# Moving three load slots 224 bytes up in each partition of a decode kernel

## The chip, the core and the metric

The kernel runs on one core of a Trainium2 chip. The metric is the device time of one execution in microseconds (us). Before the change the median of three executions is 1370.03 us, from 1369.99 to 1370.04 us.

## What is computed

One token passes through a parallel block of a transformer: layer norm, then attention over a long cache beside a gated feed-forward, and both are added to the input. Everything is fp32.

```python
xn   = layernorm(x)                                # x: [1, 1, 576]
q    = (xn @ wq).reshape(1, 1, 32, 128)            # 32 heads of 128
s    = einsum("bhqd,bhkd->bhqk", q, k_cache) * 128 ** -0.5   # k_cache: [1, 32, 16384, 128]
p    = softmax(s)
o    = einsum("bhqk,bhkd->bhqd", p, v_cache)       # v_cache: [1, 32, 16384, 128]
attn = o.reshape(1, 1, 4096) @ wo                  # wo: [4096, 576]
ffn  = (gelu(xn @ w_gate) * (xn @ w_up)) @ w_down  # 576 -> 4608 -> 576
out  = x + attn + ffn
```

There is one query, so every element of the caches is used once. K and V are 8.39 MB each for a head, 537 MB for the 32 heads; with the weights the core reads 587.6 MB from device memory.

## The kernel before

**The slots.** Nearly all that is loaded goes to three buffers of 65,536 bytes in each of the 128 partitions: two K slots (`kpool`, names `kslot`) and one V slot (`vpool`, name `vslot`). One slot holds the K or the V of one head: 128 positions of 128 floats in a partition. The slots lie one behind another. The lowest begins at byte 27,680 of the partition, the next two at 93,216 and 158,752. Below them lies the pool `cpool` with the small tiles that live for the whole program, above them `spool` with the small tiles of a head. All pools are laid out in the order in which the program opens them, each tile at the next multiple of 32 bytes.

**The loads.** Every load of a cache or a weight is issued by `load()` (L69) on SyncE's DMA queue. A transfer of a head's K or V is 128 rows, one for each partition, of 65,536 contiguous bytes each; the destination begins where the slot begins. The first head's K comes in two halves. The weights share the slots: `wq` and the feed-forward's `w_gate` and `w_up` come first (parts of `w_gate` and `w_up` in the V slot, name `mix`), `w_down` and `wo` come last. Their parts begin at places within a slot that are multiples of 256 bytes.

**The head loop** (from L249 on). For head h it issues the load of K of head h, then the load of V of head h-1, and then:

- `qk` (L215, L216): VectorE multiplies K in place by the query, which lies in all partitions in the tile `qs`, and sums over the 128 elements of each position into the scores `s`.
- `pv` of the head before (L236): 64 matmuls on TensorE with the weights of the softmax in the tile `pe` and V as the moving operand, summed in PSUM.
- `softmax` (L220 to L229): the maximum over partitions by way of TensorE, then one exponential on ScalarE, which writes `pe` and, through `accum_out`, the row sum into column h of the tile `lsum`.

A load waits on SyncE's queue until its slot is free. The V slot is free when `pv` is done. A K slot is free when `qk` of two heads earlier is done; by the order of issue that load also follows the load of V before it. The DMA queue itself works through what has been issued in order, so a load that is issued while another is still moving starts when that one is through.

**The end.** `w_down` and `wo` are loaded in pieces that get smaller, the last ones 2,304 bytes in a partition. TensorE multiplies each piece as it lands (L281), `lsum` is summed over partitions at L300, and 576 floats are written out.

**Where the small tiles lie.** `lsum` is the second last tile of `cpool` ahead of the head loop: behind it follow `oall`, three small tiles of the feed-forward's activation and three of the end (`rl`, `on`, `oT`), and behind those the slots.

```python
lsum = cpool.tile([P, H], F32, name="lsum")
oall = cpool.tile([P, H], F32, name="oall")
```

Of the kernel before, what the change touches and what calls it, by code (L numbers as in the profile page):

```python
# [8 lines left out]
F32 = mybir.dt.float32  # L9
# [4 lines left out]
P = 128  # L14
H, SK, DH = 32, 16384, 128
# [19 lines left out]
QUART = D // 4  # L35
HG = 4
PW = 4 * HG
QH = 4


@with_exitstack
def kernel(ctx: ExitStack, tc: tile.TileContext, x, k_cache, v_cache, wq, wo, wg, wu, wd, out):
    nc = tc.nc
    cpool = ctx.enter_context(tc.tile_pool(name="cpool", bufs=1))
# [17 lines left out]
    def kslot():  # L62
        return kpool.tile([P, R * DH], F32, tag="k", name="kslot")

    def vslot():
        return vpool.tile([P, R * DH], F32, tag="v", name="vslot")

    def load(dst, src):
        nc.sync.dma_start(dst, src)  # L69
        return dst  # L70
# [79 lines left out]
    def q_spread(h):  # L150
        r = 32 * (h // (H // 4))
        lo = h % (H // 4) * DH
        pq = ps_s.tile([P, 512], F32, tag="sm", name="pq")
        nc.tensor.matmul(pq, ones[r : r + 1, :], qrow[r : r + 1, lo : lo + QH * DH], start=True, stop=True)  # L154
        return pq

    def q_take(h, pq):
        qs = spool.tile([P, QH, DH], F32, name="qs", bufs=1)
        nc.scalar.activation(qs.rearrange("p h d -> p (h d)"), pq, AF.Copy)
        for i in range(QH):  # L160
            Q[h + i] = qs[:, i : i + 1, :]
# [41 lines left out]
    S, KT, VT = {}, {}, {}  # L203
    pe = cpool.tile([P, PW - 4 + 32 * PW], F32, name="pe")
    nc.vector.memset(pe, 0.0)
    pe4 = pe[:, PW - 4 :].rearrange("p (k s) -> p k s", s=PW)[:, :, :4]
    lsum = cpool.tile([P, H], F32, name="lsum")
    oall = cpool.tile([P, H], F32, name="oall")

    def qk(h, i, n):  # L210
# [21 lines left out]
    def pv(h):  # L232
        vt, i = VT.pop(h), h % HG
        for k in range(32):
            q, lo = 32 * (k % 4), k * PW + PW - 4 - 4 * i
            nc.tensor.matmul(PO[h // HG % 2][q : q + PW, :], pe[:, lo : lo + PW], vt[:, k * 512 : (k + 1) * 512],  # L236
                             start=i == 0 and k < 4, stop=i == HG - 1 and k >= 28)

    def out_heads(h):
        o4 = spool.tile([P, 512], F32, name="o4", bufs=1)  # L240
        nc.scalar.activation(o4, PO[h // HG % 2], AF.Copy)  # L241
        pc = ps_s.tile([P, 512], F32, tag="sm", name="pc")
        pick = same[:, :PW].rearrange("p (i j) -> p j i", j=4)
        for j in range(4):
# [4 lines left out]
    for h in range(H + 1):  # L249
# [4 lines left out]
        if h > 0:  # L254
            VT[h - 1] = load(vslot() if h < H else kslot(), vv[h - 1])
        more = (h + 1) % QH == 0 and h + 1 < H
        pq = q_spread(h + 1) if more else None
# [100 lines left out]
```

## Time and profile before

| what | value |
|---|---|
| median of 3 executions | 1370.03 us |
| the profiled execution's own time | 1370.16 us |
| its span, first to last instruction | 1368.3 us |
| VectorE busy | 1135.8 us (83%) |
| TensorE matmuls busy | 406.0 us (30%) |
| mean busy share of the 16 DMA engines | 9 tenths or more in 39 of 40 slices |
| bytes moved by DMA, mean rate | 588.00 MB, 430 GB/s |
| packets on the loads' queue | 11,664 |

The span leaves 1.86 us of the profiled execution outside it. An engine is busy while one of its instructions runs; idle time of an engine that is not the bottleneck costs nothing. A packet of the DMA queue is one contiguous row of a transfer, or a four-byte one that tells a semaphore that an engine's part is done. A rate taken over a short stretch is rough, since a packet's bytes are put down to its own time.

### The profile page before, as it was taken

To read this page: it belongs to the slowest core of one execution; us is meant where nothing else is said; L and a number is where in the kernel's file an instruction comes from. 1 tells how busy PE (TensorE), PEld (TensorE's weight loads), DVE (VectorE), ACT (ScalarE), POOL (GpSimd) and SP (SyncE) were. 2 spreads that over 40 slices of the span, in tenths; PEclk is the share of its full clock that TensorE was granted. 3 is DMA by queue.
4 is the path that set the end of the run, shared out by engine and by line. 5 is a ranking of instruction groups with operands and counts; after the bars stand their busy time and mean duration, and the time that the engine had idled before them with its cause. 6 is when DMAs were issued, how large, how long until landed. Compare 5 with 4: busy or idle time off the path is not lost.

```text
span 1368.3 us, 6377 instructions
## 1 busy us (share of the span) xinstructions
PE 406.0 (30%) x2870; PEld 118.1 (9%) x2870; DVE 1135.8 (83%) x169; ACT 36.5 (3%) x126; POOL 1.0 (0%) x7
## 2 busy tenths in 40 slices
PE   4321233322311232323212332322213333221156
PEld 1110000100000000100000000100001000000012
DVE  1069999899888888898888888998888888988840
ACT  0000000000000000000000000000000000000000
POOL 0000000000000000000000000000000000000000
PEclk8775565565556556565566566565556555665577
DMA  9999999999999999999999999999999999999997
GB/s 404 440 425 450 430 429 430 430 435 432 437 435 429 431 430 439 432 432 435 431 436 433 433 431 430 435 432 439 435 430 430 431 432 437 438 435 428 429 428 336
DMA packets 11704, 588.00 MB, mean 430 GB/s; under 512 B 1303, under 2 KB 1309, under 8 KB 1694
## 3 DMA queue, kind: packets, MB, share of 16 engines
q1 hardware_dynamic: 11664, 587.60, 99.4%
q8 instruction: 22, 0.36, 0.1%
q14 instruction: 4, 0.03, 0.0%
q10 hardware_dynamic: 14, 0.01, 0.0%
HBM read 587.60 MB, written 0.00 MB: 429 GB/s over the span
## 4 chain that ended last, share of the span: by engine, by line
DMA 51%; DVE 46%; PE 2%; issue 0%; SPq 0%; ACT 0%; DVEq 0%
DMA kslot<-in_A_k_cache_dram 41%; DVE s L216 23%; DVE kslot L215 23%; DMA kslot<-in_A_v_cache_dram 3%; DMA kslot<-in_B_w_up_dram 3%; DMA kslot<-in_A_wo_dram 3%; DMA kslot<-in_A_wq_dram 2%; PE pg L139 1%; PE po L236 1%; DVE gu L179 0%; SPq L69 0%; PE pt L222 0%; DVE vslot L176 0%; DVE pm L220 0%; DVE nm L224 0%
## 5 line engine op out<-in xcount | busy, mean ns | idle before, releaser
L215 DVE TENSOR_TENSOR kslot<-kslot,qs 128x16384 f32<-128x16384 f32 (+1 forms) x33 | 551.3, 16705 | 88.4 <-DMA kslot<-in_A_k_cache_dram 86.9
L216 DVE TENSOR_REDUCE s<-kslot 128x128 f32<-128x16384 f32 (+1 forms) x33 | 551.2, 16703 | 3.3
L236 PE MATMUL po<-vslot,pe 128*16 128x512 f32 x1984 | 286.1, 741 | 645.0 <-DMA vslot<-in_A_v_cache_dram 645.0
L236 PEld LDWEIGHTS po<-vslot,pe 128*16 128x16 f32 x1984 | 67.3, 113 | 848.2 <-issue 848.2
L222 PE MATMUL pt<-ident,pm 128*1 128x128 f32 x32 | 11.9, 372 | 236.0 <-DVE pm L220 236.0
L176 DVE TENSOR_TENSOR vslot<-pg,same 128x396 f32<-128x396 f32 (+1 forms) x6 | 3.0, 552 | 69.1 <-PE pg L139 69.1
L139 PE MATMUL pg<-kslot,xnb 128*32 128x396 f32 (+2 forms) x208 | 23.6, 615 | 33.6 <-DMA kslot<-in_B_w_gate_dram 18.9
L228 ACT ACTIVATE nb<-pb 128x1 f32<-128x1 f32 x32 | 5.5, 171 | 812.4 <-PE pb L226 812.4
L320 DVE TENSOR_TENSOR x<-x,po 64x288 f32<-64x288 f32 x1 | 0.5, 457 | 30.8 <-PE po L281 30.8
L222 PEld LDWEIGHTS pt<-ident,pm 128*1 128x1 f32 x32 | 2.5, 79 | 259.4 <-DVE pm L220 218.5
L226 PE MATMUL pb<-nm,ones 1*128 1x1 f32 x64 | 18.1, 350 | 13.2 <-DVE nm L224 13.2
L224 DVE TENSOR_REDUCE nm<-pt 1x1 f32<-1x128 f32 x32 | 8.9, 278 | 14.9 <-PE pt L222 14.9
L226 PEld LDWEIGHTS pb<-nm,ones 1*128 1x128 f32 x64 | 15.8, 305 | 22.2 <-DVE nm L224 11.3
L154 PE MATMUL pq<-qrow,ones 1*128 1x512 f32 x16 | 15.6, 1073 | 0.0
L229 ACT ACTIVATE pe<-s,nb 128x128 f32<-128x128 f32 x32 | 12.8, 401 | 1.0
L302 DVE RECIPROCAL rl<-pl 128x32 f32<-128x32 f32 x1 | 0.4, 358 | 14.9 <-PE pl L300 14.9
L281 PE MATMUL acc<-kslot,oT 128*1 128x144 f32 (+1 forms) x112 | 10.5, 376 | 6.7 <-DMA kslot<-in_A_wo_dram 6.7
L139 PEld LDWEIGHTS pg<-kslot,xnb 128*32 128x32 f32 x208 | 7.1, 126 | 51.0 <-DMA kslot<-in_B_w_gate_dram 19.7
L241 ACT ACTIVATE o<-po 128x512 f32<-128x512 f32 x8 | 4.8, 597 | 222.0 <-PE po L236 222.0
L236 PE MATMUL po<-kslot,pe 128*16 128x512 f32 x64 | 9.6, 769 | 2.6 <-DMA kslot<-in_A_v_cache_dram 2.6
L281 PE MATMUL acc<-vslot,hT 128*1 128x288 f32 x56 | 8.6, 473 | 5.6 <-DMA vslot<-in_B_w_down_dram 5.6
L245 PE MATMUL pc<-same,o 128*128 128x4 f32 x64 | 8.4, 255 | 5.7 <-ACT o L241 5.7
(74 smaller groups left out, 109.9 us busy)
## 6 DMA issues: line engine op xcount, KB each, us to landing
kslot<-in_A_k_cache_dram SPq DMA_DIRECT2D x2, 4096.0 KB
vslot<-in_B_w_down_dram SPq DMA_DIRECT2D x1, 8064.0 KB
kslot<-in_B_w_gate_dram SPq DMA_DIRECT2D x1, 6912.0 KB, 54.0
kslot<-in_B_w_up_dram SPq DMA_DIRECT2D x1, 6912.0 KB
kslot<-in_A_wo_dram SPq DMA_DIRECT2D x1, 4608.0 KB, 39.2
vslot<-in_B_w_gate_dram SPq DMA_DIRECT2D x1, 2304.0 KB, 28.9
vslot<-in_B_w_up_dram SPq DMA_DIRECT2D x1, 2304.0 KB, 37.6
kslot<-in_B_w_down_dram SPq DMA_DIRECT2D x1, 2304.0 KB, 28.7
```

The costliest lines, as they stand in the source:

```text
L139: nc.tensor.matmul(pg[32 * q : 32 * q + 32, b, :size], lhs, rhs[:, lo : lo + size], start=k == 0, stop=k == len(steps) - 1)
L154: nc.tensor.matmul(pq, ones[r : r + 1, :], qrow[r : r + 1, lo : lo + QH * DH], start=True, stop=True)
L215: tc.keep_in_program_order(nc.vector.tensor_mul(blk, blk, Q[h].to_broadcast([P, n, DH])))
L216: nc.vector.tensor_reduce(S[h][:, i : i + n], blk, axis=AX.X, op=ALU.add)
L222: nc.tensor.transpose(pt[:1, :P], pm, ident)
L224: tc.keep_in_program_order(nc.vector.tensor_reduce(nm, pt[:1, :P], axis=AX.X, op=ALU.max, negate=True))
L226: nc.tensor.matmul(pb[:, :1], ones[:1, :], nm, start=True, stop=True)
L228: nc.scalar.activation(nb, pb[:, :1], AF.Copy, scale=SCALE)
L229: nc.scalar.activation(pe4, S.pop(h).rearrange("p (k s) -> p k s", s=4), AF.Exp, bias=nb, scale=SCALE, accum_out=lsum[:, h : h + 1])
L236: nc.tensor.matmul(PO[h // HG % 2][q : q + PW, :], pe[:, lo : lo + PW], vt[:, k * 512 : (k + 1) * 512], start=i == 0 and k < 4, stop=i == ...
L245: nc.tensor.matmul(pc[:, :HG], o4[:, j * DH : (j + 1) * DH], pick[:, j, :], start=j == 0, stop=j == 3)
L281: nc.tensor.matmul(g, lhs, w[:, i * n : (i + 1) * n], start=id(g) not in seen, stop=last)
```

## The change

The tile `lsum` is made 56 floats (224 bytes) longer in each partition, and the program goes on using its first 32 columns alone. What is allocated behind it moves up by 224 bytes: in `cpool` the tile `oall` and the six small ones named above, then the three slots, and above them `spool`. The lowest slot begins at byte 27,904, the others at 93,440 and 158,976. 27,680 is 108 x 256 + 32, and 27,904 is 109 x 256. The distances between the slots, and between the slots and the tiles of `spool`, stay as they are. No instruction is added or taken away, and none changes its order or its size.

```diff
@@ -35,6 +35,7 @@
 QUART = D // 4
 HG = 4
 PW = 4 * HG
+PAD = 56
 QH = 4
 
 
@@ -204,7 +205,7 @@
     pe = cpool.tile([P, PW - 4 + 32 * PW], F32, name="pe")
     nc.vector.memset(pe, 0.0)
     pe4 = pe[:, PW - 4 :].rearrange("p (k s) -> p k s", s=PW)[:, :, :4]
-    lsum = cpool.tile([P, H], F32, name="lsum")
+    lsum = cpool.tile([P, H + PAD], F32, name="lsum")[:, :H]
     oall = cpool.tile([P, H], F32, name="oall")
 
     def qk(h, i, n):
```

## The prediction

> **What bounds the kernel now.** I read the page first: what is busy, and what the chain that ended last is made of.
>
> ```profile
> span 1368.3 us, 6377 instructions
> PE 406.0 (30%) x2870; PEld 118.1 (9%) x2870; DVE 1135.8 (83%) x169; ACT 36.5 (3%) x126; POOL 1.0 (0%) x7
> DMA  9999999999999999999999999999999999999997
> q1 hardware_dynamic: 11664, 587.60, 99.4%
> DMA 51%; DVE 46%; PE 2%; issue 0%; SPq 0%; ACT 0%; DVEq 0%
> ```
>
> The loads' queue keeps the 16 DMA engines at work for 99.4% of the span. The chain gives VectorE (DVE) nearly half of the path, so the second question is whether VectorE is a bound of its own. The chain in order of time, around one pair of heads in the middle, shows how the two alternate:
>
> ```profile
> 420.40 42.77 DMA kslot<-in_A_k_cache_dram
> 463.19 17.24 DVE kslot L215
> 480.52 17.23 DVE s L216
> 497.77 42.84 DMA kslot<-in_A_k_cache_dram
> ```
>
> From one K load on this chain to the next are 497.77 - 420.40 = 77.37 us, two heads. In that time four transfers of 8.39 MB pass, 33.55 MB, so 434 GB/s. The chain runs back through VectorE only because a K load is issued when VectorE frees the slot. The load isn't late for that: it is issued at 459.05 us, as the timeline has it, while the V load before it lands at 482.66 us, so it has been queued 23.6 us before the engines can start it. Similarly V is issued at 453.86 us, and K lands at 463.17 us: 9.3 us to spare. The waits of 420 to 498 us say the same from the other side:
>
> ```profile
> PE po L236 <- DMA vslot<-in_A_v_cache_dram: 43.8, 2, 21.9
> DVE kslot L215 <- DMA kslot<-in_A_k_cache_dram: 6.1, 2, 3.1
> ```
>
> VectorE waits some 3.1 us for K in each head, TensorE 21.9 us for V. So a head takes what its bytes take, and VectorE is second by 3.1 us of 38.7.
>
> Next, busy times by stage: where VectorE hardly works, where it works without a break, and two pairs of heads in the loop (columns: stretch, its length, busy time of each engine with its instructions, clock, DMA share, GB/s).
>
> ```profile
> 25.00:83.00 58.00, 32.77 (x306) 10.59 (x306) 4.59 (x6) 2.90 (x3) 0.00 (x0) 0.78 1.01 433
> 83.00:122.00 39.00, 0.00 (x0) 0.00 (x0) 38.47 (x14) 0.23 (x1) 0.00 (x0) 0.52 1.01 434
> 420.40:497.80 77.40, 21.00 (x134) 5.63 (x134) 70.05 (x9) 1.33 (x6) 0.00 (x0) 0.59 1.00 433
> 886.60:964.00 77.40, 20.75 (x134) 5.58 (x134) 70.05 (x9) 1.33 (x6) 0.00 (x0) 0.61 1.00 433
> ```
>
> The last columns are what matters: 433 to 434 GB/s, whether VectorE is busy for 4.59 of 58 us or for 38.47 of 39. The engines' work doesn't slow the transfers here.
>
> **What a row of a transfer costs.** The change can reach the time through the destination address of the loads, so I take the cost of one row apart. The queue's 11,664 packets are, by the trace's packet records, 10,368 rows of data and 1,296 packets of 4 bytes. On each of the 16 engines that is 648 rows. All rows go to a slot at a place that is 32 bytes past a multiple of 256. Their median durations:
>
> | row, bytes | rows | median ns |
> |---|---|---|
> | 65,536 | 8,192 | 2,421 |
> | 32,768 | 256 | 1,216 |
> | 9,216 | 384 | 351 |
> | 4,608 | 128 | 181 |
> | 2,304 | 256 | 95 |
> | 4 | 1,296 | 9 |
>
> From 32,768 to 65,536 bytes the time grows by 1,205 ns, which is 0.03677 ns for a byte (27.2 bytes per ns, 435 GB/s for 16 engines). At that price 65,536 bytes are 2,410 ns, so 11 ns of a row don't go with its length. For 4,608 bytes it is 181 - 169 = 12 ns, for 2,304 bytes 95 - 85 = 10 ns, and the 4-byte packet, with no row to speak of, takes 9 ns.
>
> **The change, part by part.**
>
> *Loads to the moved slots.* Where a row begins can't change what a byte costs in its middle, since the 32,768 and 65,536-byte rows have the same begin and end and differ by bytes alone; what it can change is the share per row. The lower bound of a gain is 0, the upper one the whole 11 ns: 648 x 11 ns = 7.1 us. The nearest row is the 4-byte packet: 9 ns are there without a row, so 11 - 9 = 2 ns are left for a begin and an end off the boundary. I take half of them, 1 ns, because part of these 2 ns is the rounding of the records: 648 x 1 ns = 0.65 us less. All of it lies on the path, since the engines never stand still. In the other direction the bound is set by the records as well: of the 8,192 long rows 5,907 take 2,418 to 2,422 ns and 2,264 take 2,425 to 2,428 ns. Were all of the first kind to become like the second, 7 ns each, the time would be 648 x 7 ns = 4.5 us longer. No reason in the trace excludes that, so it stays as the upper end of the range of this cost.
>
> The Trainium skill has a rule on this, in "DMA: Bandwidth & Descriptors", How a descriptor splits into AXI transactions: a descriptor that doesn't start at a multiple of 256 bytes gets a first transaction from the boundary below, and the bytes ahead of its start cost beats of 32 bytes all the same. By it a row of 65,536 bytes at offset 32 has 2,049 beats and an aligned one 2,048; the estimate from the page's beat and the row's price per byte is 1.2 ns a row, 0.8 us in all, 1369.3 us. The records' 2 ns neither show nor exclude it. A second rule speaks against more than that: the same page, Where 436 GB/s comes from, puts the ceiling of the ports at 435.2 GB/s, and the trace's 435 from the two row lengths agrees; by it the kernel has no faster rate to go to.
>
> *VectorE, TensorE and ScalarE on moved tiles.* The same instructions read the slots 224 bytes higher. L215 and L216 take 17.23 and 17.22 us in every full head for 16,384 elements, 1.05 ns an element, and I cost the move at nothing. The work that covers an error is the load itself: VectorE has 3.1 us a head to spare, so L215 and L216 together would have to become 9% slower (3.1 of 34.45 us) before a head got longer. Below that a slower or faster VectorE changes nothing. TensorE's 64 matmuls at L236 (8.7 to 9.9 us a head) have the 9.3 us by which V is queued early.
>
> *`lsum`, `oall` and the small tiles.* ScalarE writes a column of `lsum` with each exponential (0.40 us a head, off the path), L300 reads it at the end (0.39 us), while `w_down` is still on its way. No instruction more, no wait more, no other order: nothing.
>
> The sum is made against the profiled execution: 1370.16 - 0.65 = 1369.51 us. It lies 0.13 us above the median of the runs, so the forecast is 1369.4 us. A difference under 0.2%, 2.7 us here, is about what a measurement of this kernel can tell from no change; it is 4.2 ns per row.
>
> **The rivals.**
>
> *Aligned rows lose most of their fixed share: faster.* If it is the begin off the boundary that makes most of the 11 ns, on the write side for instance by an extra transaction at either end, a row gets 4.2 to 11 ns shorter. For it: this share is there in every row, and nothing hides it. Against it: the 4-byte packet pays 9 ns too, and a transfer's rows go through one after another. At 7 ns: 648 x 7 = 4.5 us, 1365.5 us; at the bound of 11 ns 7.1 us, 1362.9 us. It needs over 4.2 ns to count as faster.
>
> *Rows become slower at the new place: slower.* The place is the write of a row to a slot while VectorE goes through the other K slot in place. Rows that begin at a multiple of 256 in all partitions could meet these accesses, or each other, at the same bank or port, as the slow kind of rows may already do. Price: every row of the fast kind becomes one of the slow kind, 7 ns by 648, +4.5 us, 1374.5 us; it decides from 4.2 ns a row. For it: rows of two kinds show that something besides bytes acts on a row. Against it: the rate in the stage without VectorE is that of the stage with it, and the slots keep their distances from each other and from the tiles of `spool`, so who meets whom on the way changes little.
>
> *VectorE becomes the bound: slower.* If the reads at the new place cost it over 9%, a head takes VectorE's time. At 12% it would be 34.45 x 0.03 = 1 us a head beyond the cover, 32 us in 31 heads, over 1400 us. Nothing in the trace speaks for it: its instructions work at one speed in both K slots. I give it a small part of the chance.
>
> *The slots don't move.* Then the time stays at 1370.0 us; in the result it can't be told from the forecast and is counted with it.
>
> **How the numbers follow.** Within 0.2% (the forecast, with the case that nothing moves): 0.53, likeliest at 1369.4 us, its own range 1367.3 to 1372.7. Faster through the fixed share: 0.28. Slower by rows 0.16 and by VectorE 0.03, together 0.19. Eight in ten are held by the first two cases, so the range goes from 1363.0, the whole fixed share gone, to 1372.8, the edge of the first case; the slower cases are left out.
>
> **What would show it right or wrong.** In the profile after, rows of 65,536 bytes take 2,420 ns instead of 2,421, and the pair of heads on the chain 77.3 us, still 433 to 434 GB/s; L215 and L216 stay at 17.2 us, and the wait of L215 for K at about 3.1 us a head. Faster by the rival: rows at 2,410 to 2,417 ns, a pair of heads at 77.2 us or less, and L215's wait shorter by as much. Slower by rows: rows at 2,425 ns or more with a longer wait of L215. Slower by VectorE: L215 or L216 over 18.8 us and no wait for K. The forecast is wrong altogether if the rate in the loop leaves 432 to 435 GB/s, for then the middle of a row depends on its address after all, which the two row lengths can't show, having the same offset.

## The result: 3.5 us faster, and where the profile shows it

The changed kernel takes 1366.53 us in the median of nine runs (1366.46 to 1366.75), the kernel before beside it 1370.04 us. The ratio is 0.9975, with a 95% interval of 0.9966 to 0.9983: faster by 3.5 us, a quarter of a per cent. That is just beyond the 0.2% that the prediction counted as a difference. The range of the prediction held it; its likeliest case did not come.

The page of the changed kernel looks like that of before. These are the lines that answer to the ones shown there (every line of the kernel has moved down by one):

```profile
span 1364.7 us, 6377 instructions
PE 404.2 (30%) x2870; PEld 117.8 (9%) x2870; DVE 1135.7 (83%) x169; ACT 36.5 (3%) x126; POOL 1.0 (0%) x7
q1 hardware_dynamic: 11664, 587.60, 99.5%
DMA 51%; DVE 46%; PE 2%; issue 0%; SPq 0%; DVEq 0%; ACT 0%
```

The chain in the fourth line has the same shares, the queue is at work throughout with the same packets and bytes, and the span is 3.6 us shorter. VectorE's busy time has not moved (1135.8 to 1135.7 us). The groups by form say it of each instruction, the first line of before, the others of after:

```profile
L215 DVE TENSOR_TENSOR kslot<-kslot,qs 128x16384 f32<-128x16384 f32 x31 | 533.9, 17223 | 88.4 <-DMA kslot<-in_A_k_cache_dram 86.9 <-ACT pe L229 1.5
L216 DVE TENSOR_TENSOR kslot<-kslot,qs 128x16384 f32<-128x16384 f32 x31 | 533.9, 17223 | 83.8 <-DMA kslot<-in_A_k_cache_dram 83.8
L217 DVE TENSOR_REDUCE s<-kslot 128x128 f32<-128x16384 f32 x31 | 533.8, 17220 | 3.2
```

The products and the sums have the 17,223 and 17,220 ns that they had before. What shrank is VectorE's idle time, span less busy time, from 232.5 to 229.0 us: 3.5 us. Most of it is the wait for K ahead of the products, 86.9 us over the program before and 83.8 us after (with what is put down to `pe`, 88.4 and 83.8 us). In the feed-forward 1.4 us come back: there VectorE waits 70.5 us for TensorE's sums, 69.1 us before. The waits of one pair of heads and the stretches by stage are too coarse to show it:

```profile
PE po L237 <- DMA vslot<-in_A_v_cache_dram: 43.5, 2, 21.8
DVE kslot L216 <- DMA kslot<-in_A_k_cache_dram: 6.0, 2, 3.1
419.30:496.60 77.30, 20.95 (x134) 5.64 (x134) 70.05 (x9) 1.33 (x6) 0.00 (x0) 0.59 1.00 433
884.30:961.60 77.30, 20.16 (x134) 5.48 (x134) 70.03 (x10) 1.33 (x6) 0.00 (x0) 0.61 1.00 433
```

6.1 to 6.0 us, and 433 GB/s as before. It takes a longer stretch of the chain. Here are two K loads twelve heads apart, first of before, then of after (start, length, what):

```profile
654.19 42.84 DMA kslot<-in_A_k_cache_dram
1118.82 44.41 DMA kslot<-in_A_k_cache_dram
652.49 42.71 DMA kslot<-in_A_k_cache_dram
1116.13 44.11 DMA kslot<-in_A_k_cache_dram
```

Before, twelve heads take 1118.82 - 654.19 = 464.63 us, after it 1116.13 - 652.49 = 463.64 us. The 0.99 us between them, over 12 x 16 = 192 rows that each engine writes in that time, are 5.2 ns a row. Such a stretch is good to some 0.3 us, 1.6 ns a row, as the kernels further down show; the rows themselves say it more closely.

The trace's packet records show them. Before, the 65,536-byte rows came in kinds: 2,418 to 2,422 ns, and 2,264 of them at 2,425 to 2,428 ns. After it 8,026 of 8,192 take 2,418 ns, and those at 2,425 ns or more are no longer a kind. From the start of one row to the start of the next on its engine it was 2,420.0 ns on the mean of the loop, and is 2,414.9 ns: 5.1 ns less (each packet followed to the one that starts where it ends, the 4-byte packets between them included, without the 42 steps in either kernel that took 0.1 us longer or more). For an engine's 648 rows that is 3.3 us, somewhat less in truth, because short rows gain less: all 256 rows of 2,304 bytes take 93 ns now, where they took 93 to 107 ns, 96.0 on the mean. The 42 long steps add to it. They stand beside packets of the queue that the page lists as `q8 instruction`, lost 29.8 us together before and lose 26.7 us after, and over 16 engines the difference is 0.2 us. The two make up nearly all of the 3.5 us.

The price is there where VectorE hardly works, too. The 256 rows of 55,296 bytes are loaded between 40 and 73 us, where VectorE is busy for 4.59 of 58 us; they took 2,045.7 ns on the mean before, and all take 2,041 ns after. So it is not a meeting of the writes with VectorE's work in the other slot.

### The profile page after: what moved, and what is told of

It is laid out like the page before. It is cut to its first block, busy times and chain, and to the rows that moved or that the text cites. A ratio compares the mean times of both kernels' runs of the same rounds, so it can differ in the third digit from the quotient of the medians.

```text
span 1364.7 us, 6377 instructions
## 1 busy us (share of the span) xinstructions
PE 404.2 (30%) x2870; PEld 117.8 (9%) x2870; DVE 1135.7 (83%) x169; ACT 36.5 (3%) x126; POOL 1.0 (0%) x7
## 4 chain that ended last, share of the span: by engine, by line
DMA 51%; DVE 46%; PE 2%; issue 0%; SPq 0%; DVEq 0%; ACT 0%
DMA kslot<-in_A_k_cache_dram 41%; DVE s L217 23%; DVE kslot L216 23%; DMA kslot<-in_A_v_cache_dram 3%; DMA kslot<-in_B_w_up_dram 3%; DMA kslot<-in_A_wo_dram 3%; DMA kslot<-in_A_wq_dram 2%; PE pg L140 1%; PE po L237 1%; SPq L70 0%; PE pt L223 0%; DVE vslot L177 0%; DVE pm L221 0%; DVE nm L225 0%; PE acc L282 0%
## 5 line engine op out<-in xcount | busy, mean ns | idle before, releaser
L216 DVE TENSOR_TENSOR kslot<-kslot,qs 128x16384 f32<-128x16384 f32 (+1 forms) x33 | 551.3, 16705 | 83.8 <-DMA kslot<-in_A_k_cache_dram 83.8
L177 DVE TENSOR_TENSOR vslot<-pg,same 128x396 f32<-128x396 f32 (+1 forms) x6 | 3.0, 551 | 70.5 <-PE pg L140 70.5
L221 DVE TENSOR_REDUCE pm<-s 128x1 f32<-128x128 f32 x32 | 9.1, 286 | 1.1
```

The costliest lines, as they stand in the source:

```text
L216: tc.keep_in_program_order(nc.vector.tensor_mul(blk, blk, Q[h].to_broadcast([P, n, DH])))
L221: tc.keep_in_program_order(nc.vector.reduce_max(pm, S[h], axis=AX.X))
```

## Which boundary: 64, 128, 256 or 1024 bytes

Two theories stood at the start. One: a row costs more when its write doesn't begin at some boundary, and the question is which. The other: the tiles beside the slots moved as well, and it is those. Four kernels ran side by side, three with the slots at other places and one with the slots left where they were.

**Slots at 64 past a multiple of 256** (the change with another number):

```diff
-PAD = 56
+PAD = 8
```

> The slots lie 32 bytes higher than before, at byte 27712: a multiple of 64, not of 128. Theory A (a row costs about 5 ns more when it begins off a 64-byte boundary): the whole gain of the change, rows at 2418 ns, 1366.5 us. Theory B (the boundary that counts is 128 or 256 bytes, as with the page's rule on transactions of 256 bytes): no gain, rows at 2421 and 2428 ns, 1370.0 us. Theory C (each 32 bytes off the next boundary costs something): part of the gain, between 1366.5 and 1370 us.

**Slots at 128 past a multiple of 256**:

```diff
-PAD = 56
+PAD = 24
```

> The slots lie 96 bytes higher than before, at byte 27776: a multiple of 128, not of 256. Theory A (64-byte boundary): 1366.5 us, as with the change. Theory B with 128 bytes: 1366.5 us, with 256 bytes: 1370.0 us.

**Slots at a multiple of 1024**, against the kernel before:

```diff
-    std = cpool.tile([1, 1], F32, name="std")
+    sr = cpool.tile([1, 2], F32, name="sr")
+    std, rstd = sr[:, 0:1], sr[:, 1:2]
...
-    rstd = cpool.tile([1, 1], F32, name="rstd")
```

> The slots lie 32 bytes lower than before, at byte 27648, a multiple of 1024; two one-element tiles (the standard deviation and its reciprocal) share one tile for that. Theory A, and theory B up to 256 bytes: 1366.5 us, the same as the change. If boundaries of 512 or 1024 bytes count as well: below 1366.2 us.

**The tiles above the slots alone**, against the kernel before; `qs` is the first tile of `spool`, and the longer `qs` moves those behind it:

```diff
-        qs = spool.tile([P, QH, DH], F32, name="qs", bufs=1)
+        qs = spool.tile([P, 56 + QH * DH], F32, name="qs", bufs=1)[:, 56:].rearrange("p (h d) -> p h d", d=DH)
```

> The slots stay at byte 27680; only the tiles above them (the query, the scores and the small ones of a head) move up by 224 bytes. If the gain comes from where the loads land: 1370.0 us. If it comes from the tiles that the engines read and write beside the slots: 1366.5 us.

The kernel before took 1370.12 us in these runs.

| slots, bytes past a multiple of 256 | median us | ratio to before, 95% interval | start to start of a row, ns |
|---|---|---|---|
| 64 | 1369.61 | 0.9995 [0.9986, 1.0004] | 2,418.9 |
| 128 | 1369.29 | 0.9994 [0.9985, 1.0003] | 2,418.8 |
| 0 (a multiple of 1024) | 1366.80 | 0.9976 [0.9966, 0.9985] | 2,414.9 |
| 32, tiles above moved | 1370.16 | 1.0000 [0.9992, 1.0009] | 2,420.0 |

The boundary is 256 bytes. 64 and 128 keep most of the price, and their intervals don't tell them from the kernel before; only their rows do, by 1 ns each. A multiple of 1024 gives what a multiple of 256 gives, and reaches it without a pad. The tiles above the slots have no part in it. The chain shows the two kinds, first twelve heads of the kernel at 128 and then twelve of the one at 1024:

```profile
653.61 43.11 DMA kslot<-in_A_k_cache_dram
1118.37 43.99 DMA kslot<-in_A_k_cache_dram
613.74 42.82 DMA kslot<-in_A_k_cache_dram
1077.64 43.85 DMA kslot<-in_A_k_cache_dram
```

464.76 us for the first, 463.90 us for the second. Over all kernels that load the K and V of these heads whole, such twelve heads take 464.6 to 464.9 us with every slot off the boundary and 463.6 to 464.0 us with every slot on it. That tells the boundary, but not 64 and 128 bytes from 32.

## Is it a price per row, and does every row pay alone?

**Every load of K and V in two**, so that the same bytes make more rows, once with the slots of before and once with those of after. The edit is the same in both:

```diff
-            for i in range(0, R, n):
-                load(KT[h][:, i * DH : (i + n) * DH], kv[h][:, i * DH : (i + n) * DH])
+            for i in range(0, R, SUB):
+                load(KT[h][:, i * DH : (i + SUB) * DH], kv[h][:, i * DH : (i + SUB) * DH])
...
-            VT[h - 1] = load(vslot() if h < H else kslot(), vv[h - 1])
+            VT[h - 1] = vslot() if h < H else kslot()
+            for i in range(0, R, SUB):
+                load(VT[h - 1][:, i * DH : (i + SUB) * DH], vv[h - 1][:, i * DH : (i + SUB) * DH])
```

> Slots as before the change, but each load of a head's K or V is issued as two, of rows of 32768 bytes: 1152 rows for an engine in place of 648. A price per row off the boundary (5.2 ns over an aligned one, which has some 5 ns of its own over its bytes) gives 504 x 10 ns = 5 us and 63 more completions of about 6 ns, 0.4 us: 1375.5 us. If the price goes with the bytes: 504 x 5 ns and the completions, 1373 us.

> The same two loads for each K and V with the slots at byte 27904, as after the change. Price per row: 504 x 5 ns + 0.4 us over the change's 1366.5 us, 1369.4 us; the distance to the run with halves off the boundary is then 1152 x 5.2 ns = 6 us, where it was 3.5 us. If the price goes with the bytes the distance stays 3.5 us.

The span and the loads' queue of the two pages, off the boundary first:

```profile
span 1373.7 us, 6462 instructions
q1 hardware_dynamic: 20736, 587.60, 99.6%
span 1367.5 us, 6462 instructions
q1 hardware_dynamic: 20736, 587.60, 99.6%
```

The bytes are those of before, the packets 20,736 for 11,664. 1375.45 us were measured off the boundary and 1369.30 us on it, where 1375.5 and 1369.4 were expected. The distance of 6.15 us is that of 1,152 rows at 5.3 ns; the rows of 32,768 bytes start 1,215.3 ns apart off the boundary and 1,210.2 ns apart on it, 5.1 ns again. So the price goes with the rows and not with the bytes.

**One kind of slot on the boundary.** For V alone a tile of 56 floats lies between the K slots and the V slot, in a pool of its own that is opened between theirs; for K alone the changed kernel gets one of 8 floats there, so that its V slot is 32 bytes off.

```diff
+    gpool = ctx.enter_context(tc.tile_pool(name="gpool", bufs=1))
     vpool = ctx.enter_context(tc.tile_pool(name="vpool", bufs=1))
...
+    gap = gpool.tile([P, 56], F32, name="gap")
+    nc.gpsimd.memset(gap, 0.0)
```

> The K slots stay at bytes 27680 and 93216, the V slot moves up by 224 bytes to a multiple of 256; an unused tile of 224 bytes, which GpSimd clears once, lies between. Of an engine's 648 rows 288 go to the V slot. If the gain is a price per row that doesn't begin at a multiple of 256 (some 5 ns each, 3.5 us for 648): 288/648 of it, 1.5 us less than before, 1368.5 us, with rows of two kinds half and half. If any slot off the boundary keeps the engines in step with it: 1370 us.

> The K slots lie at multiples of 256, the V slot 32 bytes past one; the other way round than in the run with V alone, with 360 of an engine's 648 rows on the boundary. That run gained 2.1 us where a plain price per row gave 1.5 us. Plain price per row: 360/648 of 3.5 us, 1.95 us less than before, 1368.1 us. If rows off the boundary cost less when transfers on the boundary lie between them (half, as the V run's records look): a gain of some 2.7 us, 1367.4 us.

V alone took 1367.94 us (0.9984 [0.9976, 0.9993]), 2.1 us less than the kernel before beside it, and K alone 1367.51 us (0.9982 [0.9973, 0.9990]), 2.5 us less. Together that is 4.6 us, more than the 3.5 us that both bring at once. The intervals alone don't exclude a plain price per row, 1.5 and 1.95 us: each reaches some 1.2 us either way. The records do. With V alone on the boundary rows start 2,416.1 ns apart on the mean of the loop, with K alone 2,416.0 ns, where a plain price on half the rows would give 2,417.4 ns. That is 1.2 and 1.1 ns over the changed kernel's, so 2.4 and 2.2 ns for each row off the boundary, about half of 5.1 ns. Of the sixteen rows that an engine writes for one K and one V, four as a rule take 2,419 to 2,428 ns in either kernel, in one stretch around the 4-byte packet between the two, and the others nearly all 2,418 ns. The stretch takes in rows of both transfers, so the records don't say which row pays. The sequence repeats itself after 32 rows, two heads (96% of the rows of V alone have the time of the row 32 earlier), so it is no noise; what is carried from one row to the next the records don't say.

## Write or read, and how far off

**16 bytes off a multiple of 32**, against the kernel before:

```diff
-        return kpool.tile([P, R * DH], F32, tag="k", name="kslot")
+        return kpool.tile([P, R * DH + 8], F32, tag="k", name="kslot")[:, 4 : 4 + R * DH]
...
-        return vpool.tile([P, R * DH], F32, tag="v", name="vslot")
+        return vpool.tile([P, R * DH + 8], F32, tag="v", name="vslot")[:, 4 : 4 + R * DH]
```

> Each slot is 32 bytes longer and its loads begin 16 bytes behind its start: at 48, 80 and 112 bytes past a multiple of 256, so off a multiple of 32 as well; VectorE and TensorE read them there. If all that counts is whether a row begins at a multiple of 256: as before, 1370 us. If the beat of 32 bytes counts too, one more at an end is 1.2 ns a row: 1370.8 us; if every transaction pays it (256 a row), far more: rows at 2700 ns, some 1550 us.

**224 bytes past a multiple of 256**, with the change's number at 48:

```diff
-PAD = 56
+PAD = 48
```

> The slots begin 224 bytes past a multiple of 256. By the page's beats a row of 65536 bytes then takes 7 beats more than an aligned one, where 32, 64 and 128 bytes take 1, 2 and 4: the time would be the longest of them all, 7 x 1.2 ns x 648 = 5.5 us over the aligned one, 1372 us. By what the runs at 32, 64 and 128 showed (3.5, 2.9 and 2.5 us over the aligned one, less as the offset grows): 1369 us or somewhat less.

The first took 1369.55 us (0.9997 [0.9988, 1.0006]), the second 1369.99 us (1.0000 [0.9991, 1.0009]). Rows start 2,419.1 and 2,420.0 ns apart. An address that isn't a multiple of 32 costs nothing more, and 224 bytes cost what 32 bytes cost. Over an aligned row it is 5.1 ns at 32, 4.0 at 64, 3.9 at 128 and 5.1 at 224 bytes: nearly flat, with no growth along the offset. (The expectation at 224 had carried on the fall from 32 to 128 bytes, to 1369 us or less; that was wrong.)

**The read moved instead.** Both kernels read K and V of all heads but the last from 8 floats further on; the first has the slots of before, the second those of after:

```diff
-    kv = k_cache.rearrange("b h (p n) d -> (b h) p (n d)", p=P)
-    vv = v_cache.rearrange("b h (p n) d -> (b h) p (n d)", p=P)
+    def shifted(c):
+        flat = c.rearrange("b h s d -> (b h s d)")
+        heads = [flat[h * SK * DH + 8 : (h + 1) * SK * DH + 8].rearrange("(p f) -> p f", p=P) for h in range(H - 1)]
+        return heads + [c.rearrange("b h (p n) d -> (b h) p (n d)", p=P)[H - 1]]
+
+    kv, vv = shifted(k_cache), shifted(v_cache)
```

> Slots as before the change, 32 bytes past a multiple of 256; the heads' K and V, but for the last head, are read from 32 bytes further on in device memory too (so it computes on shifted data). If what costs is the distance between the place of the read and of the write within 256 bytes: as aligned, 1366.5 us. If the write's place alone counts: as before, 1370.0 us. If the read pays a price of its own as well: 1370 to 1373.5 us.

> Slots at multiples of 256 as after the change; the heads' K and V, but for the last head, are read from 32 bytes further on in device memory (shifted data again). If the write's place alone counts: 1366.5 us. If the distance between read and write counts: 1370.0 us. If the read pays its own price: some 3 us over the change, 1370 us as well, and then the run with both shifted lies over 1370 us.

1370.05 us with both moved (1.0000 [0.9991, 1.0009]) and 1366.76 us with the read alone moved (0.9976 [0.9966, 0.9985]). The rows start 2,420.0 and 2,414.9 ns apart, as before and as after the change. So of the two places that of the write counts: to begin the read 32 bytes further on costs nothing that can be measured, and to move it along with the write brings nothing. At which address the caches themselves begin is not on record.

## Why the prediction was partly right

**What bounds the kernel: right.** The loads set the pace, the time by which rows got shorter came off VectorE's idle time and off the whole, and nothing that was queued behind it took its place. The middle of a row does not depend on the address: 433 GB/s in the same stretches, 1,205 ns from a row of 32,768 bytes to one of 65,536 before and after (2,418 - 1,213), and the halved rows pay by the row.

**VectorE and the small tiles at nothing: right.** Their durations are the same to the nanosecond, and moving the tiles above the slots alone left the time at 1370.16 us.

**The term for the loads: the mechanism was right, the size was not.** 648 rows by 1 ns were put down, 0.65 us; it was 648 by 5.1 ns, 3.3 us, and 0.2 us in the long steps, which had no term. Two things went wrong in that term. The first was the median. It was taken to stand for a row, at 11 ns over the bytes, and the 2,264 rows at 2,425 to 2,428 ns were set aside as a second kind whose cause was open; they came back only as a bound for a loss. They were the larger part of the price: off the boundary most rows take some 3 ns more than an aligned one, and these 2,264, a good quarter, 9.5 ns more. The mean of the same records, without some 20 rows in either kernel that were held up for 0.1 us or more, is 2,422.6 ns, against 2,418.1 ns after it: 4.5 ns. The rest is that one row's record overlaps the next by 3.4 ns before and by 3.9 ns after. The second was to halve a remainder of 2 ns for rounding, where nothing in the table said that it was rounding. The mean less 2,410 ns for the bytes and less the 9 ns of the 4-byte packet, which was in the table, is 3.6 ns, so 2.3 us and 1367.7 us.

**The rivals.** That rows would lose over 4.2 ns of their fixed share, at 0.28, is what happened, at 5.1 ns, near the point from which it counts. The range held the result because it took this rival in, and not by the term put down. The signs that were named for it did not come: rows were to take 2,410 to 2,417 ns and take 2,418 ns by the median, and the pair of heads on the chain, 77.37 us before, takes 77.27 us, between the 77.3 us of the forecast and the 77.2 us of the rival. One pair and a median were too coarse to tell the two apart. What spoke against it there, that the 4-byte packet pays 9 ns too, was sound: an aligned row keeps 8 ns over its bytes. It only was no argument about the rows of the slow kind. The slower case by rows had the slow kind the wrong way round: it isn't what rows could become but what they were, and it went away. VectorE never came near to being the bound: it keeps its wait of 3 us a head. The ends of the range, 1363.0 and 1372.8 us, lie 0.1 us off the 1362.9 and 1372.7 us that the prediction's own sums give, which changes nothing.

**The rule on transactions.** The Trainium skill, "DMA: Bandwidth & Descriptors", How a descriptor splits into AXI transactions, names 256 bytes as the boundary, and the runs at 64, 128, 256 and 1024 bytes agree with that. What that section of the Trainium skill says of the bytes ahead of the start is that they are fetched, which is the read. Here it was the place of the write that cost, and the read moved by 32 bytes cost nothing (1366.76 us). The Trainium skill's count of beats does not give the price: by it 32, 64, 128 and 224 bytes would cost 1, 2, 4 and 7 beats, an estimate of 1.2 to 8.2 ns a row, and the rows paid 5.1, 4.0, 3.9 and 5.1 ns. That fits one more transaction a row better than it fits beats; no record shows a transaction, so this is argued and not shown. The ceiling of 435.2 GB/s on the same page of the Trainium skill was no obstacle, because the price lay beside the bytes and not in their rate.

**What stays open:** by what mechanism a write off the boundary costs its row 4 to 5 ns, why rows of several kinds alternate there, and why they pay half when aligned transfers lie between them.

## What to carry to other kernels

Where loads set the pace, look at the address within the partition at which they are written: a buffer at a multiple of 256 bytes saved 5 ns for each long row on its engine here, and a few small tiles ahead of it decide where it lies. The gain goes with the number of rows, so it is small for rows of 64 KB (0.25%) and twice as much for halves of them (1375.45 to 1369.30 us, 0.45%). When durations come in two kinds, take the mean, and ask what the second kind is before it is set aside.

## What was not expected of the hardware

- Off the boundary, 65,536-byte rows take 2,418 to 2,422 ns mostly and 2,425 to 2,428 ns in a good quarter of the cases, in a sequence that repeats after 32 rows of an engine, four transfers (94% of the rows have the time of the row 32 earlier); on it nearly all take 2,418 ns.
- A write that begins 32 bytes off a multiple of 256 costs 5.1 ns a row, 224 bytes off the same, 64 and 128 bytes off 4 ns. A read that begins 32 bytes further on costs nothing that could be measured (1366.76 us).
- Two parts of one change brought 2.1 and 2.5 us alone and 3.5 us together, though both act on the same queue at different times; the rows bear it out, at 2.4 and 2.2 ns where both off pay 5.1 ns.
